# Attention's products with V: one run per pair of heads over all queries, and attention's tiles in rings

## The chip, the cores and the metric

The kernel runs on one core of a Trainium2 chip. The metric is the time of one execution on the device in microseconds (us); smaller is better. Executions are timed several times, and the median is given.

Five engines take part, each with its own instruction queue: TensorE (PE; its weight loads are shown as PEld), VectorE (DVE), ScalarE (ACT), GpSimd (POOL) and SyncE (SP), which here only issues DMAs.

## The reference

```
# q, k, v: (4, 8, 576, 64) float32      B, H, S, D
# M_prev: (4, 8, 64, 64), z_prev: (4, 8, 64), beta: (8,)
scores = q @ k^T / sqrt(D), causal mask
a      = softmax(scores)
local  = a @ v
q_p    = phi(q)                          # phi(x) = elu(x) + 1
mem    = (q_p @ M_prev) / (q_p @ z_prev + 1e-6)
g      = sigmoid(beta)                   # one per head
x      = g * mem + (1 - g) * local       # -> (2304 tokens, 512)
h = x @ w1_in;  y   = (h * cos(h))  @ w1_out       # 512 -> 2048 -> 512
h = y @ w2_in;  out = (h * tanh(softplus(h))) @ w2_out
```

The four weight matrices of the two FFNs come as float64, everything else as float32.

## The kernel before

**Attention.** The eight heads of a batch make four pairs, so there are 16 pairs of heads (B = 4, NP = 4). A pair's queries are done in NQ = 5 steps of 128 (the last has 64 queries, of both heads at once). The generator `attention` goes through all 80 steps, and each step passes three stages, LAGB = 2 and LAGC = 4 steps apart:

- `stage_a`: the scores of the step's queries with all keys up to them (L238, one matmul for each head, in rows 0 to 63 and 64 to 127 of the array; L251 for the last step), into the PSUM tiles sp and sd. DVE adds the mask and takes the minimum (L240, L253, L256), ACT takes the exponential and its sum (L243, L258), DVE the reciprocal (L263), and POOL or another engine scales by it and by the gate (L265). The result is the tile at.
- `stage_b`: PE transposes at, 128 keys at a time, with the identity matrix into the PSUM tile tp (L297; L303 into td for the last 64 keys of the last step). `scaled` (L112) copies tp to SBUF as aT (td as aD), on ACT (L115) and DVE (L117) in turn, in the first batch on ACT alone.
- `stage_c`: the output of the step, transposed (64 values of each of the two heads in the partitions, queries in the columns), in the PSUM tile o: the memory's term by a product with the identity (L313), then for each chunk c of 128 keys up to the diagonal and each head j a product of V with aT (L324), which fills the half j of the array's columns. ACT rounds o to float32r in xH (L328), DVE takes the rest in xL (L329); after the last step both are stored (L331, L332).

`memory` makes a pair's memory term (L277 on PE into mp, L280 to L282 on DVE, result mo) ahead of its first step. `prep` issues a pair's loads on SP's queue (kd L204, qd L206, mz L209, vt L212, qt L215) and is called at step PREP = 3 of the pair before.

A plain float32 matmul is two records of PE in the trace. A product in float32r is one record.

**The FFNs.** `ffn` is a generator of units: L420 makes h from x's two float32r parts and the weights' two, ACT, DVE and POOL make cos (L367 to L376, split in L391 and L392), and `mm2_t` makes y (L478). Tokens of a batch can start once the batch's attention has been stored. The first FFN's first half of d_ff is laid among attention's steps from the second batch on; its second half follows, then the second FFN (mish, `mm2_n`, L487). The weights are converted from float64 by `to_f32` (L121, on POOL, ACT and DVE), beginning at step CONV0 = 14 of attention.

**What sets the order.** The program is written as these generators; the scheduler of the Tile framework then sets each engine's order from the program's dependences, the buffers of each pool (BUFS) and estimates of its own. Attention's PSUM tiles have the tags S (scores) and T (all else) of one pool. A tile of a tag with n buffers waits for the release of the tile n before it.

In the trace, attention's first batch lasts to 87.7 us, where the first L420 stands; up to 131 us the first weights are still being converted; from there to 380 us attention and the first FFN's first half go side by side. The first FFN ends at 682 us, and the second takes the rest.

## Time and profile before

| what | value |
|---|---|
| time, median of 3 runs | 1071.06 us (1069.19 to 1071.45) |
| span of the profiled execution | 1068.0 us, 17139 instructions |
| PE busy | 1042.6 us (98%) |
| DVE busy | 490.7 us (46%) |
| ACT busy | 485.8 us (45%) |
| POOL busy | 391.6 us (37%) |

The profile is of one execution, whose own time is its span, 1068.0 us; the timed runs are others, and their median lies 3.1 us above the span. Busy time is the union of an engine's instructions in the trace; engines work side by side, so the shares don't add up. The rows further down give the line of the kernel, the engine, the operation and the tiles: `o<-aT,vt` is a matmul that writes o and reads aT and vt. The shape after it, as 128\*64, is the part of the array that the matmul fills, rows by columns.

### The profile page before, as it was taken

What the parts mean: (1) busy time and instruction counts of PE and PEld (TensorE: products, weight loads), DVE (VectorE), ACT (ScalarE), POOL (GpSimd) and SP (SyncE); (2) the same over time, 40 slices, a digit from 0 to 9 for tenths busy, and PEclk for the clock granted to TensorE, in tenths of its full rate; (3) what the DMA queues carried; (4) which work ended last, traced back from release to release, by engine and by line L of the source; (5) the groups of instructions that cost most, each with busy time, mean ns of one, the idle gap of its engine ahead of it and who ended that gap; (6) DMA issues with size and microseconds to landing.
All of it is one profiled execution on the core that took longest, in us unless ns stands there. A gap on an engine that the chain in (4) does not pass through costs nothing.

```text
span 1068.0 us, 17139 instructions
## 1 busy us (share of the span) xinstructions
PE 1042.6 (98%) x6512; PEld 873.7 (82%) x6512; DVE 490.7 (46%) x1136; ACT 485.8 (45%) x1023; POOL 391.6 (37%) x425
## 2 busy tenths in 40 slices
PE   6997999999999999999999999999999999999998
PEld 4666688787878899998888889888888888888897
DVE  4588885445554558776766655665000000000000
ACT  6797875556564534344535454543322321222131
POOL 3377853323232334555555555654101010110100
PEclk8999999999999999999999999999999999999999
DMA  6366642323121275425345355630300300110010
GB/s 235 119 196 224 205 135 82 119 83 122 59 87 46 73 266 190 139 90 198 110 166 177 111 176 185 228 119 22 116 1 1 118 1 0 60 40 1 21 41 20
DMA packets 66369, 116.99 MB, mean 110 GB/s; under 512 B 5616, under 2 KB 25072, under 8 KB 66288
## 3 DMA queue, kind: packets, MB, share of 16 engines
q1 hardware_dynamic: 66288, 115.91, 32.2%
q8 instruction: 51, 0.84, 0.3%
q14 instruction: 30, 0.25, 0.1%
HBM read 87.58 MB, written 28.31 MB: 109 GB/s over the span
## 4 chain that ended last, share of the span: by engine, by line
PE 92%; ACT 2%; DVE 2%; DMA 2%; issue 1%; POOL 1%; SPq 0%; DVEq 0%; POOLq 0%; ACTq 0%
PE h L420 37%; PE y L478 20%; PE y L487 18%; PE o L324 5%; PE sp L238 4%; PE tp L297 4%; PE o L313 2%; PE mp L277 1%; PE sp L251 1%; DMA qt<-in_qp_dram 1%; DMA wst<-in_w1i_dram 1%; DVE at L240 1%; ACT at L243 1%; DMA vt<-in_vn_dram 1%; POOL at L265 0%
## 5 line engine op out<-in xcount | busy, mean ns | idle before, releaser
L420 PE MATMUL h<-xbH,w 128*128 128x256 f32 (+1 forms) x1536 | 393.0, 338 | 0.1
L420 PEld LDWEIGHTS h<-xbH,w 128*128 128x128 f32 x1536 | 266.9, 190 | 33.7 <-issue 1.0
L420 PE MATMUL h<-xbL,w 128*128 128x256 f32 (+1 forms) x768 | 258.0, 336 | 1.5 <-DMA xbL<-xsL 1.5
L478 PE MATMUL y<-g,w 128*128 128x256 f32 (+1 forms) x1344 | 221.5, 319 | 4.4 <-ACT aT L115 4.2
L478 PEld LDWEIGHTS y<-g,w 128*128 128x128 f32 x1344 | 193.1, 192 | 30.8 <-issue 9.4
L487 PE MATMUL y<-w,g 128*128 128x512 f32 x864 | 201.8, 389 | 0.0
L487 PEld LDWEIGHTS y<-w,g 128*128 128x128 f32 x864 | 161.9, 188 | 33.5
L392 DVE TENSOR_TENSOR g<-e,g 128x512 fp32r<-128x512 f32 x36 | 24.9, 691 | 297.1 <-ACT g L115 297.1
L420 PEld LDWEIGHTS h<-xbL,w 128*128 128x128 f32 x768 | 145.6, 190 | 16.9 <-DMA xbL<-xsL 1.7
L392 POOL TENSOR_TENSOR g<-e,g 128x512 fp32r<-128x512 f32 x36 | 47.8, 1328 | 286.5 <-ACT g L115 286.5
L265 POOL TENSOR_SCALAR at<-at,sm,omg 128x128 f32<-128x128 f32 (+2 forms) x144 | 102.7, 723 | 134.4 <-DVE sm L263 119.2
L384 ACT ACTIVATE e<-h 128x512 f32<-128x512 f32 x72 | 43.0, 597 | 232.5 <-PE h L420 231.0
L392 POOL TENSOR_TENSOR g<-u,g 128x512 fp32r<-128x512 f32 x72 | 102.0, 1436 | 121.5 <-ACT g L115 45.6
L367 ACT ACTIVATE u<-h 128x512 int32<-128x512 f32 x72 | 42.9, 595 | 111.9 <-PE h L420 104.2
L243 ACT ACTIVATE at<-at,mn 128x128 f32<-128x128 f32 (+3 forms) x128 | 70.9, 555 | 28.2 <-DVE mn L240 26.8
L129 DVE SCALAR_TENSOR_TENSOR wst<-wst 128x512 int32<-128x512 int32 x64 | 53.9, 843 | 37.7 <-POOL wst L119 31.3
L119 POOL TENSOR_SCALAR wst<-wst 128x512 f32<-128x512 f32 x64 | 46.4, 731 | 63.2 <-DMA wst<-in_w1i_dram 25.1
L297 PE MATMUL tp<-ident,at 128*128 128x128 f32 x384 | 63.9, 285 | 5.6 <-DVE den L281 2.2
L368 DVE SCALAR_TENSOR_TENSOR u<-u,h 128x512 f32<-128x512 int32 x72 | 49.0, 682 | 40.8 <-ACT u L367 40.5
L240 DVE CUSTOM_DVE_ANT_0 at<-sp,mask 128x128 f32<-128x128 f32 (+3 forms) x128 | 59.3, 482 | 17.6 <-PE sp L238 16.0
L133 DVE TENSOR_TENSOR wst<-wst 128x512 int32<-128x512 int32 x64 | 66.1, 1035 | 1.2
L324 PE MATMUL o<-aT,vt 128*64 128x128 f32 (+1 forms) x896 | 64.5, 272 | 1.7 <-ACT aT L115 1.5
(76 smaller groups left out, 1084.1 us busy)
## 6 DMA issues: line engine op xcount, KB each, us to landing
wst<-in_w1i_dram SPq DMA_DIRECT2D x16, 512.0 KB, 5.4
wst<-in_w1o_dram SPq DMA_DIRECT2D x16, 512.0 KB, 4.6
wst<-in_w2i_dram SPq DMA_DIRECT2D x16, 512.0 KB, 4.0
wst<-in_w2o_dram SPq DMA_DIRECT2D x16, 512.0 KB, 4.7
qd<-in_qT_dram SPq DMA_DIRECT2D x16, 320.0 KB, 3.4
vt<-in_vn_dram SPq DMA_DIRECT2D x16, 320.0 KB, 3.2
xbH<-xsH SPq DMA_DIRECT2D x20, 256.0 KB, 4.9
xbL<-xsL SPq DMA_DIRECT2D x20, 256.0 KB, 4.6
```

Source lines behind the costliest of these rows:

```text
L129: nc.vector.scalar_tensor_tensor(lo, hi, 3, lo, ALU.logical_shift_left, ALU.bitwise_or)
L133: nc.vector.tensor_tensor(dst, lo, hi, ALU.bitwise_xor)
L240: nc.vector.tensor_tensor_reduce(at[:, :N], sp[:, :N], mask[:, SM - q0:SM - q0 + N], SSC, 3.0e38, ALU.add, ALU.min, mn[:, j:j + 1])
L243: marks["act"] = nc.scalar.activation(at[:, :N], at[:, :N], AF.Exp, bias=mn[:, j:j + 1], scale=-1.0, accum_out=sm[:, j:j + 1]).ins
L265: turn_of("sc", b == 0).tensor_scalar(at[:, :N], at[:, :N], sm[:, j:j + 1], gates[j], ALU.mult, ALU.mult)
L297: nc.tensor.transpose(tp[:, c:c + P], at[:, c:c + P], ident)
L324: marks["pe"] = nc.tensor.matmul(o[j * D:(j + 1) * D, :n], st["vt"][:kk, c, j * D:(j + 1) * D], a, start=False, stop=c == i, skip_group_ch ...
L368: nc.vector.scalar_tensor_tensor(u, u.bitcast(I32), -TWO_PI, h, ALU.mult, ALU.add)
L392: turn_of(kind).tensor_tensor(gL, g, gH.bitcast(F32), ALU.subtract)
L420: nc.tensor.matmul(h[:, a * T:(a + 1) * T], w_[:, c, f0:f0 + P], x_[c], start=m == 0, stop=m == 3 * NC - 1)
L478: nc.tensor.matmul(y[e // per][:, cols], w_[:, f, es], g_, start=fst and m == 0 and e % per == 0, stop=lst and m == 2, skip_group_check=True)
L487: nc.tensor.matmul(y[t], g_[:, tsl], w_[:, f, :], start=fst and m == 0, stop=lst and m == 2, skip_group_check=True)
```

## The change

The product with V is made once for each pair of heads, after its last step, and no longer in each step. For each chunk c of 128 keys, one matmul for each head takes all queries from the diagonal on: 512, 448, 320, 192 and 64 columns (L341 of the new kernel). The first 64 queries lie in a bank of their own, od, with a memory term (L327) and one product for each head (L334) of their own. The memory term of the rest is five products with the identity (L331). Two evacuations on each of ACT and DVE follow, of 64 and of 512 columns, and the two stores.

For this the transposed weights of a whole pair are kept: aTr holds two turns of two heads, in place of the seven aT buffers. The last step's transposes, which hold both heads, go into it by two copies, one for each head (ACT and DVE in turn).

The tiles kd, qd, vt, qt, ph, xH, xL and at are now each one tile with slots that are taken in turn (`ring`), and the buffers of kd, qd, aD and mo go from four to two, those of xL from three to two. The scheduler is free to set another order.

```diff
 BUFS = dict(
-    mb=2, kd=4, qd=4, aD=4, vt=2, qt=1, ph=2, den=2, mo=4, xH=1, xL=3, sm=7, mn=2, at=8, aT=7, u=2, e=3, g=4, h=4, y=4, xb=3, yp=3, yh=2, yl=2, wst=2, S=6, T=8,
+    mb=2, kd=2, qd=2, aD=2, vt=2, qt=1, ph=2, den=2, mo=2, xH=1, xL=2, sm=7, mn=2, at=8, u=2, e=3, g=4, h=4, y=4, xb=3, yp=3, yh=2, yl=2, wst=2, S=6, T=8,
 )
...
+    rings = {}
+
+    def ring(pool, tag, shape, dtype=F32):
+
+        if tag not in rings:
+            rings[tag] = [pool.tile([shape[0], BUFS[tag], *shape[1:]], dtype, name=tag), 0]
+        r = rings[tag]
+        r[1] += 1
+        return r[0][:, (r[1] - 1) % BUFS[tag]]
 
...
+        aTr = ap.tile([P, 4, NQ - 1, S], F32, name="aTr")
...
-            kd = ap.tile([P, S], F32, tag="kd", name="kd", bufs=BUFS["kd"])
+            kd = ring(ap, "kd", [P, S], F32)
...
-            vt = ap.tile([P, NQ, P], F32, tag="vt", name="vt", bufs=BUFS["vt"])
+            vt = ring(ap, "vt", [P, NQ, P], F32)
...
         def stage_b(b, p, i):
             st = prepd[b, p]
-            n = P if i < 4 else D
-            aTs = []
-            for at in st["at", i]:
+            if i == 0:
+                r = turns["aT"] = (turns.get("aT", -1) + 1) % 2
+                st["aT"] = [aTr[:, 2 * r + h] for h in range(2)]
+                st["aD"] = ap.tile([P, 2, D], F32, tag="aD", name="aD", bufs=BUFS["aD"])
+            aT = st["aT"]
+            W = min(i + 1, 4)
+            for j, at in enumerate(st["at", i]):
                 tp = bank("T", [P, SM], "tp")
-                aT = ap.tile([P, SM], F32, tag="aT", name="aT", bufs=BUFS["aT"])
-                W = P * min(i + 1, 4)
-                for c in range(0, W, P):
-                    nc.tensor.transpose(tp[:, c:c + P], at[:, c:c + P], ident)
-                scaled("aT", aT[:, :W], tp[:, :W], first=b == 0)
-                aTs.append(aT)
+                for c in range(W):
+                    nc.tensor.transpose(tp[:, c * P:(c + 1) * P], at[:, c * P:(c + 1) * P], ident)
+                tc4 = tp.rearrange("k (c q) -> k c q", q=P)[:, :W]
+                if i < 4:
+                    scaled("aT", aT[j][:, :W, i * P:(i + 1) * P], tc4, first=b == 0)
+                else:
+                    for h in range(2):
+                        scaled("aT", aT[h][:, :, SM:], tc4[:, :, h * D:(h + 1) * D], first=b == 0)
             if i == 4:
-                aD = ap.tile([P, 2, D], F32, tag="aD", name="aD", bufs=BUFS["aD"])
                 tp = bank("T", [P, SM], "td")
                 nc.tensor.transpose(tp[:D, :P], at[:, SM:], ident)
-                scaled("aD", aD.rearrange("p a b -> p (a b)")[:D, :P], tp[:D, :P])
-                aTs.append(aD)
-            st["aT", i] = aTs
-
-        def stage_c(b, p, i):
+                scaled("aD", st["aD"].rearrange("p a b -> p (a b)")[:D, :P], tp[:D, :P])
+
+        def stage_c(b, p):
             st = prepd[b, p]
-            n = P if i < 4 else D
-            q0 = i * P
-            o = bank("T", [P, P], "o")
-            nc.tensor.matmul(o[:, :n], st["mo"][:, i], ident[:, P - n:], start=True, stop=False,
-                             skip_group_check=True)
-            for c in range(i + 1):
-                kk = P if c < 4 else D
+            aT, aD, vt = st["aT"], st["aD"], st["vt"]
+            od = bank("T", [P, D], "od")
+            o = bank("T", [P, SM], "o")
+            nc.tensor.matmul(od, st["mo"][:, 0], ident[:, :D], start=True, stop=False, skip_group_check=True)
+            for c in range(NQ):
+                r0, n = (D, D) if c == 0 else (0, P) if c < 4 else (0, D)
+                i0 = r0 if c < 4 else P - D
+                nc.tensor.matmul(o[:, c * P + r0 - D:c * P + r0 - D + n], st["mo"][:, c], ident[:, i0:i0 + n],
+                                 start=c == 0, stop=False, skip_group_check=True)
+            for j in range(2):
+                nc.tensor.matmul(od[j * D:(j + 1) * D, :], vt[:D, 0, j * D:(j + 1) * D], aT[j][:D, 0, :D],
+                                 start=False, stop=True, skip_group_check=True)
+            for c in range(NQ):
+                q0 = max(c * P, D)
                 for j in range(2):
-                    if i < 4:
-                        a = st["aT", i][j][:, c * P:(c + 1) * P]
-                    elif c < 4:
-                        a = st["aT", i][0][:, c * P + j * D:c * P + (j + 1) * D]
-                    else:
-                        a = st["aT", i][1][:D, j]
+                    kk = P if c < 4 else D
+                    a = aT[j][:, c, q0:] if c < 4 else aD[:D, j]
                     marks["pe"] = nc.tensor.matmul(
-                        o[j * D:(j + 1) * D, :n], st["vt"][:kk, c, j * D:(j + 1) * D], a,
-                        start=False, stop=c == i, skip_group_check=True).ins
-            xH = st["xH"]
-            nc.scalar.activation(xH[:, q0:q0 + n], o[:, :n], AF.Copy)
-            nc.vector.tensor_tensor(st["xL"][:, q0:q0 + n], o[:, :n], xH[:, q0:q0 + n].bitcast(F32), ALU.subtract)
-            if i == 4:
-                nc.sync.dma_start(xsH[p, :, b * S:(b + 1) * S], xH.bitcast(F32))
-                marks["sp"] = nc.sync.dma_start(xsL[p, :, b * S:(b + 1) * S], st["xL"].bitcast(F32)).ins
-                del prepd[b, p]
+                        o[j * D:(j + 1) * D, q0 - D:], vt[:kk, c, j * D:(j + 1) * D], a,
+                        start=False, stop=c == NQ - 1, skip_group_check=True).ins
+            xH, xL = st["xH"], st["xL"]
+            for t, q0, q1 in ((od, 0, D), (o, D, S)):
+                nc.scalar.activation(xH[:, q0:q1], t, AF.Copy)
+                nc.vector.tensor_tensor(xL[:, q0:q1], t, xH[:, q0:q1].bitcast(F32), ALU.subtract)
+            nc.sync.dma_start(xsH[p, :, b * S:(b + 1) * S], xH.bitcast(F32))
+            marks["sp"] = nc.sync.dma_start(xsL[p, :, b * S:(b + 1) * S], xL.bitcast(F32)).ins
+            del prepd[b, p]
 
...
             if 0 <= s - LAGC < ns:
-                stage_c(*steps[s - LAGC])
+                if steps[s - LAGC][2] == NQ - 1:
+                    stage_c(*steps[s - LAGC][:2])
```

The new lines that the prediction names: L249 and L262 are the scores (L238 and L251 before), L310 the transposes (L297), L331 and L327 the memory term (L313), L341 and L334 the products with V (L324), L438 the first FFN's h (L420), L505 the second FFN's y (L487). The number of L324's 480 matmuls becomes 192.

**The order on PE, in the first pairs.** Before, at the first pair of heads, transposes of softmax weights into tp, the memory term (`o<-ident,mo`) and the products with V (`o<-aT,vt`) take turns, a step at a time:

```order
L297 MATMUL tp<-ident,at 128x128 x6
L313 MATMUL o<-ident,mo 128x128
L324 MATMUL o<-aT,vt 64x128
L297 MATMUL tp<-ident,at 128x128 x3
L324 MATMUL o<-aT,vt 64x128
L297 MATMUL tp<-ident,at 128x128 x3
L313 MATMUL o<-ident,mo 128x128
L324 MATMUL o<-aT,vt 64x128 x4
L297 MATMUL tp<-ident,at 128x128 x8
L277 MATMUL mp<-mz,ph 128x130 x5
```

In the new kernel a whole pair's products stand in one run, and a long run of transposes behind it:

```order
L310 MATMUL tp<-ident,at 128x128 x2
L327 MATMUL od<-ident,mo 128x64
L334 MATMUL od<-aTr,vt 64x64 x2
L331 MATMUL o<-ident,mo 128x64
L331 MATMUL o<-ident,mo 128x128 x3
L331 MATMUL o<-ident,mo 128x64
L341 MATMUL o<-aTr,vt 64x512 x2
L341 MATMUL o<-aTr,vt 64x448 x2
L341 MATMUL o<-aTr,vt 64x320 x2
L341 MATMUL o<-aTr,vt 64x192 x2
L341 MATMUL o<-aD,vt 64x64 x2
L310 MATMUL tp<-ident,at 128x128 x18
```

What stood between the transposes now stands behind them, and the transposes of the next pair, which need only free banks and the scaled weights, have moved together.

**The order on PE, among the first FFN's matmuls.** Before, between two groups of L420 (not shown) stood pieces of two steps:

```order
L297 MATMUL tp<-ident,at 128x128 x4
L303 MATMUL td<-ident,at 64x128
L238 MATMUL sp<-kd,qd 128x256 x2
L313 MATMUL o<-ident,mo 128x128
L324 MATMUL o<-aT,vt 64x128 x8
L297 MATMUL tp<-ident,at 128x128 x2
L238 MATMUL sp<-kd,qd 128x384 x2
L313 MATMUL o<-ident,mo 128x64
L324 MATMUL o<-aT,vt 64x64 x8
L324 MATMUL o<-aD,vt 64x64 x2
```

Here is one of the new runs, with the scores (`sp`, `sd`) of the last step of the next pair in it:

```order
L331 MATMUL o<-ident,mo 128x64
L341 MATMUL o<-aTr,vt 64x512
L310 MATMUL tp<-ident,at 128x128 x4
L262 MATMUL sp<-kd,qd 128x512
L262 MATMUL sd<-kd,qd 128x64
L341 MATMUL o<-aTr,vt 64x512
L341 MATMUL o<-aTr,vt 64x448 x2
L341 MATMUL o<-aTr,vt 64x320 x2
L341 MATMUL o<-aTr,vt 64x192 x2
L341 MATMUL o<-aD,vt 64x64 x2
L249 MATMUL sp<-kd,qd 128x128 x2
L249 MATMUL sp<-kd,qd 128x256 x2
```

The two heads' products of 512 columns, which would lie side by side in the array, are parted by the transposes and the scores; the products of the other chunks stand together.

**The order on DVE, at a last step's copies.** DVE copies half of the aT tiles. Before, after the first batch, the copy of a last step's tile waits for PE alone (in brackets the engines whose signals an instruction waits for), and the score reductions (`at,mn<-sp,mask`) and the conversion of weights (wst) stand behind it:

```order
L117 COPY aT<-tp 128x512 [waits PE_49]
L117 COPY aD<-td 64x128 [waits PE_49]
L329 TENSOR_TENSOR xL<-o,xH 128x128 [waits Activation_49]
L282 TENSOR_TENSOR mo<-mp,den 128x384 [waits DVE_49]
L282 TENSOR_TENSOR mo<-mp,den 128x256 [waits DVE_49]
L263 RECIPROCAL sm<-sm 128x2 [waits Activation_49]
```

In the new kernel DVE copies one head's half (128x4x64) of the last step's tile:

```order
L126 COPY aD<-td 64x128 [waits PE_49]
L139 TENSOR_SCALAR wst<-wst 128x512 [waits DVE_49]
L251 ISA at,mn<-sp,mask 128x512 [waits PE_49]
L251 ISA mn 128x1
L274 RECIPROCAL sm<-sm 128x2 [waits Activation_49]
L126 COPY aTr<-tp 128x4x64 [waits Activation_49]
L251 ISA at,mn<-sp,mask 128x512 [waits PE_49]
L251 ISA mn 128x1
L142 TENSOR_TENSOR wst<-wst 128x512 [waits DVE_49]
```

That copy waits for ACT, which copies the other head's half of the same bank ahead of it. On SP's queue the second pair's qt moves from the 16th place to the 13th.

## Rows read from the trace of the kernel before

**Rows 1.** The page: busy time of the engines; the chain that ended last, by engine.

```profile
PE 1042.6 (98%) x6512; PEld 873.7 (82%) x6512; DVE 490.7 (46%) x1136; ACT 485.8 (45%) x1023; POOL 391.6 (37%) x425
...
PE 92%; ACT 2%; DVE 2%; DMA 2%; issue 1%; POOL 1%; SPq 0%; DVEq 0%; POOLq 0%; ACTq 0%
```

**Rows 2.** Stretches: length, busy PE, PEld, DVE, ACT, POOL; granted clock; DMA share, GB/s.

```profile
24.00:87.00 63.00, 61.85 (x504) 41.88 (x503) 47.65 (x179) 52.62 (x165) 33.70 (x44) 1.00 0.50 160
87.00:131.00 44.00, 36.88 (x298) 27.68 (x294) 37.50 (x117) 33.32 (x88) 34.11 (x37) 0.96 0.62 207
131.00:380.00 249.00, 244.82 (x2088) 204.71 (x2085) 134.82 (x455) 142.69 (x361) 82.23 (x107) 0.99 0.28 89
380.00:682.00 302.00, 301.75 (x1786) 269.42 (x1785) 204.70 (x269) 136.30 (x198) 161.42 (x140) 1.00 0.49 169
100.00:105.00 5.00, 1.84 (x20) 1.30 (x19) 5.00 (x13) 4.97 (x9) 1.80 (x2) 0.98 0.41 120
104.00:109.00 5.00, 4.17 (x40) 3.47 (x40) 5.00 (x14) 3.06 (x7) 3.85 (x3) 0.66 0.42 118
```

**Rows 3.** PE's waits, 0 to 170 us: total us, times, longest.

```profile
PE sp L238 <- DMA kd<-in_kT_dram: 4.5, 1, 4.5
```

**Rows 4.** PE's waits, 170 to 440 us.

```profile
PE y L478 <- ACT aT L115: 4.2, 3, 1.4
```

**Rows 5.** The timeline of PE, 298 to 303 us: start, length, records.

```profile
298.44 0.49 PE L313 MATMUL o<-ident,mo 128*128 128x128 f32 x2
298.86 1.09 PE L324 MATMUL o<-aT,vt 128*64 128x128 f32 x16
299.89 0.44 PE L297 MATMUL tp<-ident,at 128*128 128x128 f32 x2
300.25 0.92 PE L238 MATMUL sp<-kd,qd 64*128 64x384 f32 x4
301.10 0.43 PE L313 MATMUL o<-ident,mo 128*128 128x64 f32 x2
301.47 0.69 PE L324 MATMUL o<-aT,vt 128*64 128x64 f32 x16
302.08 0.33 PE L324 MATMUL o<-aD,vt 64*64 64x64 f32 x4
```

**Rows 6.** The timeline of PE, 41.5 to 52 us.

```profile
42.23 0.88 PE L324 MATMUL o<-aT,vt 128*64 128x128 f32 x12
43.04 0.66 PE L297 MATMUL tp<-ident,at 128*128 128x128 f32 x4
...
45.35 0.91 PE L238 MATMUL sp<-kd,qd 64*128 64x384 f32 x2
46.19 0.43 PE L313 MATMUL o<-ident,mo 128*128 128x64 f32 x2
...
50.55 0.44 PE L324 MATMUL o<-aT,vt 128*64 128x128 f32 x4
50.92 1.12 PE L251 MATMUL sp<-kd,qd 128*128 128x512 f32 x2
```

**Rows 7.** The timeline of all engines, 199 to 205 us.

```profile
200.06 1.28 ACT L243 ACT_TABLE_LOAD   x1
...
201.35 0.72 ACT L243 ACTIVATE at<-at,mn 128x512 f32<-128x512 f32 x1
...
202.94 0.47 ACT L115 ACTIVATE aT<-tp 128x384 f32<-128x384 f32 x1
...
203.46 1.79 PE L478 MATMUL y<-g,w 128*128 128x256 f32 x8 [1.39 <-ACT aT L115]
```

**Rows 8.** Groups of instructions: number | busy us, mean ns | idle before, releaser.

```profile
L324 PEld LDWEIGHTS o<-aT,vt 128*64 128x64 f32 x896 | 44.7, 139 | 14.9 <-ACT aT L115 3.6 <-issue 1.7 <-ACT xH L328 0.8
L329 DVE TENSOR_TENSOR xL<-o,xH 128x128 fp32r<-128x128 f32 (+1 forms) x80 | 21.4, 272 | 23.2 <-ACT xH L328 22.8
L328 ACT ACTIVATE xH<-o 128x128 fp32r<-128x128 f32 (+1 forms) x80 | 20.1, 256 | 16.4 <-PE o L324 14.8 <-PE h L420 1.0 <-DMA xsH<-xH 0.3
```

More of the change, by code (lines that the diff above doesn't have):

```diff
@@ L195, in bank @@
             return pools[0].tile(shape, F32, tag=tag, name=name, bufs=BUFS[tag])
+        aTr = ap.tile([P, 4, NQ - 1, S], F32, name="aTr")
+        turns = {}
         pairs = [(b, p) for b in range(B) for p in range(NP)]
@@ L201, in prep @@
             st = {}
-            kd = ap.tile([P, S], F32, tag="kd", name="kd", bufs=BUFS["kd"])
+            kd = ring(ap, "kd", [P, S], F32)
             nc.sync.dma_start(kd, kT[b, p])
-            qd = ap.tile([P, S + D], F32, tag="qd", name="qd", bufs=BUFS["qd"])
+            qd = ring(ap, "qd", [P, S + D], F32)
             nc.sync.dma_start(qd, qT[b, p])
@@ L210, in prep @@
             st["mz"] = mz
-            vt = ap.tile([P, NQ, P], F32, tag="vt", name="vt", bufs=BUFS["vt"])
+            vt = ring(ap, "vt", [P, NQ, P], F32)
             nc.sync.dma_start(vt, vn[b, p])
             st["vt"] = vt
-            qt = ap.tile([P, S], F32, tag="qt", name="qt", bufs=BUFS["qt"])
+            qt = ring(ap, "qt", [P, S], F32)
             nc.sync.dma_start(qt, qp[b, p])
-            ph = ap.tile([P, S], F32, tag="ph", name="ph", bufs=BUFS["ph"])
+            ph = ring(ap, "ph", [P, S], F32)
             nc.scalar.activation(ph, qt, AF.Relu, scale=-1.0)
@@ L220, in prep @@
             st["ph"] = ph
-            st["xH"] = ap.tile([P, S], F32R, tag="xH", name="xH", bufs=BUFS["xH"])
-            st["xL"] = ap.tile([P, S], F32R, tag="xL", name="xL", bufs=BUFS["xL"])
+            st["xH"] = ring(ap, "xH", [P, S], F32R)
+            st["xL"] = ring(ap, "xL", [P, S], F32R)
             prepd[b, p] = st
@@ L231, in stage_a @@
             mn = ap.tile([P, 2], F32, tag="mn", name="mn", bufs=BUFS["mn"])
-            ats = [ap.tile([P, S], F32, tag="at", name="at", bufs=BUFS["at"]) for _ in range(2 if i < 4 else 1)]
+            ats = [ring(ap, "at", [P, S], F32) for _ in range(2 if i < 4 else 1)]
             if i < 4:
```

## The prediction

> **What bounds the kernel now.** I read the page first. TensorE (PE) is busy 98% of the span, and the chain that ended last is 92% PE [rows 1]. A busy PE is not yet the bound, so I went to the stages. From 24 to 87 us PE idles 1.1 us of 63, from 131 to 380 us it idles 4.2 of 249, from 380 to 682 us 0.3 of 302 [rows 2]. Only from 87 to 131 us, where the first weights are converted, it idles 7.1 of 44, and there DVE is busy 37.5 and POOL 34.1 us. So in three of the four stretches whatever PE no longer does comes off the end; in the fourth it may turn into waiting. The list of PE's waits agrees: at the start 4.5 us for the first keys [rows 3], in 170 to 440 us only 4.2 us, three waits of 1.4 us each for an ACT copy of transposed weights (aT) [rows 4].
>
> Then I read attention's work on PE row by row, to see what its time is made of. All its matmuls but the transposes are plain float32, which PE runs as two records. A V-product fills half of the array's columns (128\*64 in the rows), the two heads' products start together, and so do the two heads' scores (64\*128, half of the rows).
>
> From start to start a run of 16 records lasts 1.03 us [rows 5], one of 12 lasts 0.81, one of 4 lasts 0.37 [rows 6]. Four more records (both heads, 128 columns) therefore cost **0.22 us**, and a run pays 0.15 us beside. The run of 16 records with 64 columns lasts 0.61 us [rows 5]: less the 0.15 that is 0.115 per four records, half of 0.22. Time follows the columns streamed, so weight loads, whose length doesn't depend on them, are hidden inside a run.
>
> **The price of a change of shape.** From the start of the L313 at 298.44 to that at 301.10 us are 2.66 us [rows 5]. Streaming alone is 0.22 (L313) + 0.87 (16 records) + 0.22 (two transposes, taken as 128 columns each like L313's records) + 0.66 (scores, 384 columns, both heads) = 1.97. The other 0.69 us are four changes between the full array and a half: 0.17 each. From V's side: 0.15 in the run, and L313 ahead of the run of 16 takes 0.42 in place of 0.22, of which I give half to the change before it: 0.25 to 0.35 for two changes. I take **0.16 us**, with 0.13 and 0.175 as bounds.
>
> **The price of a half alone.** One head's score of 384 columns by itself lasts 0.84 us, from 45.35 to 46.19 [rows 6]; both heads together lasted 0.85 [rows 5]. So where the order parts the two heads, the second costs as much again: 0.22 us for each 128 columns.
>
> **The change on PE.** Its products stream the same columns: per head 1,600 of V (before 128 x (1+2+3+4) + 64 x 5; after 64 + 512 + 448 + 320 + 192 + 64), and 576 of the memory term, in six matmuls in place of five. Eighteen V matmuls per pair of heads go, 288 in all; by the 64-column run that is worth nothing by itself. What moves is how often the array changes shape and how often heads are parted; both are counted in the two orders.
>
> - Changes of shape: 290 before, 219 after. 71 x 0.16 = **-11.4 us** (-9.2 to -12.4).
> - Scores whose heads are parted: 12 pairs with 4,096 columns before, 18 with 6,144 after. 2,048 / 128 x 0.22 = **+3.5 us**.
> - V-products parted: 6 with 768 columns before; after, 5 of 512 columns and 2 of 64. 1,920 / 128 x 0.22 = **+3.3 us**; the order shown with the change has one such place, where transposes and scores stand between the two products of 512.
>
> Sum on PE: -4.6 us.
>
> **The other engines.** Each pair's five evacuations on ACT and five on DVE become two and two. ACT's 80 xH take 0.26 us each, DVE's 80 xL 0.27 [rows 8]: 20.1 and 21.4 us. After: per pair one of 64 columns (at most the mean, 0.26) and one of 512, which I bound by 0.26 and 0.7, the length of ACT's 512-wide exponentials [rows 7]. At 0.7, 15.4 us each: some 5 us less on either engine. The copies of step 4's transposes become two per pair; sixteen more at 0.47 (a 384-wide copy [rows 7]) are 7.5 us over ACT and DVE at most. PE's busy rows cover all of this; uncovered, between 87 and 131 us, it is at most a quarter of either, under 2 us, of both signs. I take nothing.
>
> The rings with fewer buffers (kd, qd 4 to 2) let SP issue the third pair's keys only after the first pair's last score; behind them in SP's queue stand the next qt, mz and kd, and PE's memory term waits for these. V's next load waits for a longer run of products than before. Work for at least one whole pair lies between such an issue and its need: I take nothing, and bound it by the one such wait that the trace shows, 4.5 us [rows 3]. On the other side the second pair's qt now stands 13th in SP's queue, not 16th: a gain of nothing, or of up to the 4.5 us of [rows 3] at the start, which I leave in a rival.
>
> **A new wait.** DVE's half of step 4's copy now waits for ACT's half of the same bank, and PE's first long product needs both. Behind DVE's copy stand its score reductions and weight conversions; behind PE's product stands everything. ACT's queue can be long: from the table load at 200.06 to the aT copy that PE waited for, 3.4 us pass [rows 7]. In the new order two to five us of PE work mostly lie between those transposes and the product that needs them, so I price it at nothing in the sum.
>
> **Two rules weighed against the rows.** The 64-column run halves with its columns [rows 5], so loads don't show. The Trainium skill (TensorE: Matmul & The Clock Gate, "What overlaps and what doesn't") says that a weight load overlaps running matmuls only where its row group differs; the two heads share theirs, so no load would be hidden. By it the 576 loads that go would save more: 896 such loads are 44.7 us of load time [rows 8], 576 of them 29 us, and the sum would be near -33. By the rows it stays -4.6. I give the rule 0.03.
>
> The granted clock is 1.00 from 24 to 87 us [rows 2], in which transposes stand among everything else, and it dips to 0.66 from 104 to 109 us, after PE had worked 1.84 of the 5 us before [rows 2]. The same page ("PE-mode transpose") says that transposes don't count as activity for the clock; the new order has runs of 16 and 18 of them where the old had 8 at most. No run of that length is in this trace.
>
> **Rivals.**
> 1. *Swallowed.* Ahead of the first FFN matmul the array changes shape 83 times before and 71 after, though one more pair's scores stand there now. So much of the saving falls into attention's first batch, which feeds the stretch from 87 to 131 us, where PE waits for converted weights. If it waits as much longer as it was sooner there, 4.6 us shrink to 2 or nothing: 1069 to 1073. For it: DVE 85% busy there. Against: PE's idle is 1.1 us in the 63 us before, so PE's work sets when that stretch is reached.
> 2. *Slower: the run stands for its copies.* Each pair's run has one place to stand, for the ACT-then-DVE copy, at about 1.4 us, the length of the three waits in [rows 4]. Four such waits more than now eat the 4.6 us, five make it slower by over 0.2%; at nine of sixteen runs it is 12.6 - 4.6 = 8 us slower, 1079. For it: five of the new order's runs are broken up at just this product. Against: ACT sits idle over 40% of 131 to 380 us [rows 2].
> 3. *More.* The three waits of [rows 4] were for banks behind ACT's table loads; a new order can lose them (-4.2), and start sooner: 1058 to 1062.
> 4. *Clock.* If a long run of transposes brings the clock to half as at 104 us, a dip costs 0.34 x 5 = 1.7 us; with one in each of four early pairs 6.8 - 4.6 = +2.2: 1073.
>
> **How the numbers follow.** The span before is 1068.0 us; the median of the timed runs is 3.1 us above it. 1068.0 - 4.6 = 1063.4; with the 3.1 that is **1066.5 us**. Chances: the sum as it stands 0.42 (by its bounds 1064 to 1069); swallowed 0.22; slower 0.15; more 0.14; clock 0.04; loads (some 1040) 0.03. A measurement tells 0.2%, some 2 us, from no change. Faster: 0.40 of the first, with "more" and "loads", 0.57. Slower: "slower", a little of "swallowed" and of "clock", 0.20. The same: 0.23. The range from 1058 to 1076 leaves out the loads and the far part of "slower".
>
> **What would show it.** Two heads' products of 512 columns in 0.9 us, together; attention's last product and the last stage's first matmul (L505) some 5 us earlier; changes of shape at 0.16 us. Wrong would be: PE waits on aTr at L341; heads' products that follow each other, which would be 2.75 us more per pair, 44 in all; more idle between the first FFN matmuls.

## The result, and the profile after

The changed kernel takes **1079.86 us** (median of 4 runs, 1078.54 to 1081.43), the kernel before 1071.26 us (4 runs beside it). The ratio is **1.0081, interval 1.0065 to 1.0098**: 8.6 us slower, where 4.6 us faster was forecast, and outside the range from 1058 to 1076. The profiled execution of after has a span of 1079.2 us, 11.2 us more than that of before.

The page of after, its engines and its chain, beside [rows 1]:

```profile
span 1079.2 us, 16070 instructions
PE 1047.4 (97%) x5968; PEld 860.8 (80%) x5968; DVE 496.2 (46%) x1094; ACT 479.2 (44%) x983; POOL 391.9 (36%) x425
...
PE 82%; DVE 5%; DMA 5%; POOL 3%; ACT 3%; issue 2%; SPq 0%; POOLq 0%; DVEq 0%; ACTq 0%
```

PE has 4.8 us more busy time for less work, and 10% of the chain has moved from PE to the engines that it waits for. The stretches of [rows 2] say where (length, busy PE, PEld, DVE, ACT, POOL, granted clock, DMA share, GB/s; the last cut at 420 and 478 us):

```profile
24.00:87.00 63.00, 59.74 (x360) 37.52 (x359) 42.58 (x162) 49.16 (x154) 33.01 (x44) 0.92 0.46 146
87.00:131.00 44.00, 41.50 (x260) 28.41 (x259) 36.41 (x111) 28.94 (x81) 25.34 (x30) 0.92 0.64 206
131.00:380.00 249.00, 245.22 (x1733) 193.21 (x1732) 140.47 (x435) 143.03 (x339) 91.15 (x113) 0.99 0.31 99
...
420.00:478.00 58.00, 50.94 (x394) 49.96 (x393) 49.34 (x63) 21.32 (x30) 30.84 (x29) 0.94 0.41 125
```

The same 58 us of before:

```profile
420.00:478.00 58.00, 57.75 (x457) 56.33 (x456) 42.54 (x69) 21.82 (x32) 32.13 (x33) 1.00 0.41 139
```

Read two columns together, PE's busy time and the granted clock. From 24 to 131 us PE is busy 2.5 us more than before, but at 0.92 of the clock and not at 1.00 and 0.96. The table sums windows of half a us in the two executions. Idle is the window less PE's busy time. What the clock takes is an estimate: busy time times what the clock lacks of 1.

| us | before | after | difference |
|---|---|---|---|
| last product with V starts | 379.2 | 380.1, with 5 more FFN matmuls (0.6) done | +0.3 at equal work |
| of it PE idle | 21.5 | 20.7 | -0.8 |
| of it lost to the clock | 6.2 | 11.9 | +5.7 |
| the rest: PE's work at full clock | 351.6 | 347.5 - 0.6 | **-4.7** |
| 380 to 480 us: idle and clock | 0.2 + 0 | 7.5 + 3.1 | **+10.4** |

In these two executions PE's work shrank by about what was forecast (4.6), attention ended no sooner, and 10.4 us were lost where no line of the code was changed: the first FFN behind attention. L505 starts at 693.3 us, before (L487) at 682.0.

The loss behind attention is the larger, and e1 below takes most of it away. The figures for attention hold for these two executions only. PE's order in e1, e10 and e14 below is that of after, record for record, until well past the last product with V. There the last product starts at 380.2, 374.9 and 376.4 us, the clock takes 12.1, 5.6 and 8.2 us, and the rest is 347.4, 349.5 and 348.5 us. The rows of e10 for the first two stretches, to be read beside those of after above; then the last product of e10 and that of after (each with the lines of its own kernel):

```profile
24.00:87.00 63.00, 59.51 (x377) 38.17 (x376) 45.00 (x172) 51.49 (x162) 34.53 (x46) 0.97 0.53 163
87.00:131.00 44.00, 41.39 (x258) 28.63 (x257) 37.88 (x116) 29.83 (x80) 27.09 (x31) 0.96 0.62 199
```

```profile
374.81 0.33 PE L350 MATMUL o<-aD,vt 64*64 64x64 f32 x4
```

```profile
379.96 0.33 PE L341 MATMUL o<-aD,vt 64*64 64x64 f32 x4
```

So one order on PE ended attention anywhere from 0.4 us later than before to 4.9 us sooner at equal work, and most of the difference is the clock. The execution of before was itself one with little lost to the clock: its mean granted clock was 0.993, where the runs of before beside the experiments have 0.991 on the mean.

The waits of PE from 0 to 380 us in after (total, times, longest):

```profile
PE tp L310 <- DVE mn L251: 4.4, 4, 2.3
PE tp L310 <- DVE mo L293: 3.3, 1, 3.3
PE o L341 <- ACT aTr L124: 2.9, 1, 2.9
...
PE od L327 <- ACT aTr L124: 0.8, 1, 0.8
```

Of sixteen runs of products one stood for its copy (L341), and one stood at its start for a bank that ACT's copy frees (L327), not nine. The three waits of [rows 4] are gone. From 380 to 700 us:

```profile
PE y L496 <- POOL g L410: 5.0, 4, 2.4
PE y L496 <- DVE g L126: 2.2, 1, 2.2
```

Before, one wait of 0.2 us stood there. The largest, on POOL's timeline (start, length) and then on PE's:

```profile
463.94 0.66 POOL L128 TENSOR_SCALAR wst<-wst 128x512 f32<-128x512 f32 x1 [4.03 <-DMA wst<-in_w1i_dram]
467.99 0.64 POOL L128 TENSOR_SCALAR wst<-wst 128x512 f32<-128x512 f32 x1 [3.39 <-DMA wst<-in_w1o_dram]
468.59 0.65 POOL L128 TENSOR_SCALAR w<-wst 128x512 fp32r<-128x512 f32 x1
469.20 1.70 POOL L410 TENSOR_TENSOR g<-u,g 128x512 fp32r<-128x512 f32 x1
```

```profile
468.17 0.36 PE L496 MATMUL y<-g,w 128*128 128x256 f32 x1 [2.17 <-DVE g L126]
470.95 8.58 PE L496 MATMUL y<-g,w 128*128 128x256 f32 x47 [2.43 <-POOL g L410]
```

POOL stands 3.39 us in front of a weight piece that has not landed; the split of g (L410) stands behind it in POOL's queue, and PE's y behind that. The order of POOL's instructions at this place, before and after:

```
before                                   after
L119 TENSOR_SCALAR wst<-wst x2           L128 TENSOR_SCALAR wst<-wst x2
L119 TENSOR_SCALAR w<-wst                L128 TENSOR_SCALAR w<-wst
L163 TENSOR_TENSOR w<-wst,w              L410 TENSOR_TENSOR g<-u,g
L392 TENSOR_TENSOR g<-u,g x2             L172 TENSOR_TENSOR w<-wst,w
                                         L410 TENSOR_TENSOR g<-u,g
```

Before, this group repeats from 429 to 482 us and the two splits follow the pieces together; after, the last step of a piece stands between the two. The code there is the same.

### The profile page after: what moved, and what is told of

Same layout as the page of the kernel before. It is cut to its first block, busy times and chain, and to the rows that moved or that the text cites. A ratio compares the mean times of both kernels' runs of the same rounds, so it can differ in the third digit from the quotient of the medians.

```text
span 1079.2 us, 16070 instructions
## 1 busy us (share of the span) xinstructions
PE 1047.4 (97%) x5968; PEld 860.8 (80%) x5968; DVE 496.2 (46%) x1094; ACT 479.2 (44%) x983; POOL 391.9 (36%) x425
## 4 chain that ended last, share of the span: by engine, by line
PE 82%; DVE 5%; DMA 5%; POOL 3%; ACT 3%; issue 2%; SPq 0%; POOLq 0%; DVEq 0%; ACTq 0%
PE h L438 33%; PE y L505 18%; PE y L496 16%; PE o L341 4%; PE sp L249 4%; PE tp L310 3%; DMA wst<-in_w1i_dram 3%; DMA wst<-in_w1o_dram 2%; PE o L331 1%; POOL at L276 1%; PE mp L288 1%; DVE wst L138 1%; DVE wst L139 1%; PE sp L262 1%; POOL w L172 1%
## 5 line engine op out<-in xcount | busy, mean ns | idle before, releaser
L438 PE MATMUL h<-xbH,w 128*128 128x256 f32 (+1 forms) x1536 | 392.2, 338 | 1.4 <-DVE mo L293 1.0
L438 PEld LDWEIGHTS h<-xbH,w 128*128 128x128 f32 x1536 | 266.1, 189 | 38.2 <-DVE wst L139 2.0
L438 PE MATMUL h<-xbL,w 128*128 128x256 f32 (+1 forms) x768 | 258.1, 336 | 0.0
L505 PE MATMUL y<-w,g 128*128 128x512 f32 x864 | 201.8, 389 | 0.0
L505 PEld LDWEIGHTS y<-w,g 128*128 128x128 f32 x864 | 161.9, 188 | 33.4
L410 DVE TENSOR_TENSOR g<-e,g 128x512 fp32r<-128x512 f32 x36 | 25.9, 719 | 289.1 <-ACT g L124 289.1
L438 PEld LDWEIGHTS h<-xbL,w 128*128 128x128 f32 x768 | 145.6, 190 | 15.1
L410 POOL TENSOR_TENSOR g<-e,g 128x512 fp32r<-128x512 f32 x36 | 47.3, 1314 | 276.9 <-ACT g L124 276.9
L410 POOL TENSOR_TENSOR g<-u,g 128x512 fp32r<-128x512 f32 x72 | 102.2, 1436 | 108.8 <-ACT g L124 38.4
L254 ACT ACTIVATE at<-at,mn 128x128 f32<-128x128 f32 (+3 forms) x128 | 71.4, 560 | 22.0 <-DVE mn L251 18.3
L137 ACT ACTIVATE wst<-wst,c_seven 128x512 int32<-128x512 uint32 x64 | 49.2, 770 | 68.6 <-DMA wst<-in_w1o_dram 19.5
L249 PE MATMUL sp<-kd,qd 64*128 64x256 f32 (+3 forms) x256 | 67.4, 502 | 5.3 <-DMA kd<-in_kT_dram 4.7
L251 DVE CUSTOM_DVE_ANT_0 at<-sp,mask 128x128 f32<-128x128 f32 (+3 forms) x128 | 59.7, 484 | 27.1 <-PE sp L249 14.7
L310 PE MATMUL tp<-ident,at 128*128 128x128 f32 x384 | 62.2, 286 | 9.2 <-DVE mn L251 4.4
```

The lines of the kernel that those rows point to most:

```text
L137: nc.scalar.activation(lo, lo.bitcast(U32), AF.Relu, scale=-(2.0 ** -29), bias=c_seven)
L249: nc.tensor.matmul(sp[:, :N], st["q"][rows, q0:q0 + P], st["k"][rows, :N], start=True, stop=True)
L251: nc.vector.tensor_tensor_reduce(at[:, :N], sp[:, :N], mask[:, SM - q0:SM - q0 + N], SSC, 3.0e38, ALU.add, ALU.min, mn[:, j:j + 1])
L254: marks["act"] = nc.scalar.activation(at[:, :N], at[:, :N], AF.Exp, bias=mn[:, j:j + 1], scale=-1.0, accum_out=sm[:, j:j + 1]).ins
L310: nc.tensor.transpose(tp[:, c * P:(c + 1) * P], at[:, c * P:(c + 1) * P], ident)
L410: turn_of(kind).tensor_tensor(gL, g, gH.bitcast(F32), ALU.subtract)
```

## Experiments on the stretch behind attention

**e1: the changed kernel with the old order there.** Edges of order (which make an instruction queue behind another and wait for nothing) chain the 208 instructions of POOL, DVE and ACT behind attention's last store; ORDER lists them as the kernel before issues them.

```diff
+    for e, order in ORDER.items():
+        ins = [i for i in traced if i.engine == getattr(mybir.EngineType, e)]
+        for a, b in zip(order, order[1:]):
+            tc.add_manual_dep(ins[b], ins[a].name, mybir.DependencyInfo(
+                mybir.DependencyClass.NoSync, mybir.DependencyReason.DATA), reason="order")
```

> The changed kernel, with POOL, DVE and ACT made to issue their 208 instructions behind attention's last store (conversion of the second half of the first weights, the first FFN's cosine and split) in the order in which the kernel before issues them. Nothing else differs. Theory A: the 10.9 us that the changed kernel loses between 420 and 478 us come from that order, which the change moved along without touching the code; attention itself is neither faster nor slower. Then 1079.9 - 10.5 = about 1069.5, between 1068 and 1071.5. Rival B: the new run of products is what is slow (its waits, its evacuations, fewer buffers), and what is seen behind attention is its aftermath: then 1078 to 1081.

Measured: 1073.99 us, ratio 1.0016 (1.0000 to 1.0032). Of the 0.81% some 0.65% go, about 7 us, with nothing touched but the order of unchanged instructions. Theory A holds in part: the time lies above its 1068 to 1071.5 and well under rival B's 1078 to 1081. PE still idles 2.2 us there and the clock lacks 1.7. (The expectation speaks of 10.9 us lost in this stretch; by the rows shown it is 7.1 of idle and 3.1 of clock.)

```profile
420.00:478.00 58.00, 55.84 (x427) 54.41 (x426) 38.86 (x65) 20.49 (x29) 27.92 (x29) 0.97 0.39 120
```

**e2: the kernel before with the new order there.** The same edges, with the list of the changed kernel.

> The other way round: the kernel before, with POOL, DVE and ACT made to issue the same 208 instructions behind attention in the order in which the changed kernel issues them. Theory A: PE waits for the split of g as it does in the changed kernel, 1071.3 + 10 = 1079 to 1083. Rival B: the order is harmless where attention is the old one, 1070 to 1073.

Measured: 1073.52 us, 1.0021 (1.0006 to 1.0036): some 2 us slower, far from the 10 of theory A and more than B's none. The order costs 2 us beside the old attention and 7 beside the new: so the order alone is not the whole cause. That its cost hangs on when loads and units arrive in it is a guess; no run settles it.

**e14, e10, e15: all five engines, and an earlier load.** e14 adds PE and SP to the list; e10 also lets the first two loads of weights go ahead of the last stores; e15 does that to the kernel before.

```diff
-    with tc.issue_after(marks["pe"]), tc.issue_after(marks["sp"]):
+    with tc.issue_after(marks["pe"]):
```

> The changed kernel with the order of the kernel before on all five engines behind attention, as e10, but the first loads of weights behind the last stores. Theory A: the conversion's later start is what e1 still lost: as e1, 1072 to 1075. Rival: it was the order on PE and SP: as e10, 1068 to 1071.

> The changed kernel with the order behind attention of the kernel before on all five engines, and the first two loads of weights of that stretch ahead of the last two pairs' stores on SP's queue. In e1 (three engines' order) 4.5 to 5 us were still lost behind attention, waits and the half clock behind one of them. Theory A: they come from the conversion starting 0.8 us later against PE (first load at 382.2, before at 381.4 us), so that each load lands after POOL's turn: with the earlier load the stretch loses under 2 us, 1068 to 1072. Rival (what is lost there has another source): as e1, 1072 to 1076.

> The kernel before with its own order behind attention, and the first two loads of weights ahead of the last pairs' stores, as in e10. Its trace shows 0.2 us of waiting behind attention, so there is nothing to gain: 1069 to 1072. Were it faster than that, e10 would owe its gain to the load and not to a loss that it takes back.

Measured: e14 1072.19 us, 1.0010 (0.9995 to 1.0026); e10 1069.96 us, 1.0000 (0.9983 to 1.0017); e15 1071.75 us, 1.0004 (0.9989 to 1.0019). The load by itself gives the kernel before nothing. The changed kernel comes level with before; e1, e14 and e10 lie within each other's intervals, so which of the two edits took the last 4 us is not resolved. The times of e14 and e10 lie in the ranges of their theories A.

**e5, e6: a third staging slot**, order left free.

```diff
-    mb=2, kd=2, qd=2, aD=2, vt=2, qt=1, ph=2, den=2, mo=2, xH=1, xL=2, sm=7, mn=2, at=8, u=2, e=3, g=4, h=4, y=4, xb=3, yp=3, yh=2, yl=2, wst=2, S=6, T=8,
+    mb=2, kd=2, qd=2, aD=2, vt=2, qt=1, ph=2, den=2, mo=2, xH=1, xL=2, sm=7, mn=2, at=8, u=2, e=3, g=4, h=4, y=4, xb=3, yp=3, yh=2, yl=2, wst=3, S=6, T=8,
```

> The changed kernel with three staging slots for weights in conversion (wst) in place of two; the order is left free. Theory A: behind attention POOL stands in front of a weight piece whose load was issued late because both slots were taken, and the split of g, for which PE waits, stands behind it in POOL's queue. A third slot lets the load run ahead: the 10.9 us between 420 and 478 us shrink to 3 or less, 1069 to 1073. Rival (the conversion's own work on DVE and POOL is what is too long, not its slots): 1077 to 1081.

> The kernel before with three staging slots, as the other side of e5. The trace of before shows no wait behind attention that a third slot could take away, and PE's work in attention is 1.6 us less in the new order as I count it: 1068 to 1073 by either theory.

Measured: e5 1080.88 us, 1.0078 (1.0060 to 1.0096); e6 1084.76 us, 1.0110 (1.0092 to 1.0128). Both expectations of mine fell. With one more buffer the scheduler set another order everywhere: the last product of e6 starts at 385.7 us (before 379.2), and behind it 6.5 us more go to idle and clock. The pair says nothing of slots. A small edit moved this kernel by 13 us; that its order did it is not shown here, since no run holds e6's order, but e13 below shows it for another edit.

## Experiments on the parts of the change

**e9: rings alone.** The tiles and buffers of the change (kd, qd, aD, mo and xL at two, aT kept at seven), with stage_b and stage_c as before and the old order behind attention.

```diff
...
-            kd = ap.tile([P, S], F32, tag="kd", name="kd", bufs=BUFS["kd"])
+            kd = ring(ap, "kd", [P, S])
```

> The kernel before with only the second half of the change: kd, qd, vt, qt, ph, xH, xL and at as rings, two buffers of kd, qd, aD and mo, two of xL; the products with V are the old ones, a step at a time, and the order behind attention is that of the kernel before on POOL, DVE and ACT. If the rings cost nothing, as I priced them: 1070 to 1074. If the fewer buffers are what makes PE wait in attention: 1076 to 1081. I count 1.5 us more work on PE in the new order.

**e13: the same with the old order** on PE, DVE, ACT and POOL, all instructions, by the edges of e1.

> e9's kernel (rings and fewer buffers, products a step at a time), with every instruction of PE, DVE, ACT and POOL in the order of the kernel before; SP's loads are ordered freely. Theory A: fewer buffers make nothing wait; what made e9 9 us slower is the other order that they led to. Then as the kernel before, 1069 to 1073. Rival: a load or a tile of the rings comes free too late: 1076 to 1082.

Measured: e9 1080.59 us, **1.0090** (1.0073 to 1.0107); e13 1070.43 us, **0.9991** (0.9978 to 1.0004). These two are the clearest pair of the study: same instructions, same tiles, same buffers, ten us apart by order. Beside products a step at a time, rings and fewer buffers cost nothing, as priced; what they led the scheduler to do cost as much as the whole change. In e9 the loss lies in attention, whose last product starts at 388.5 us; PE waits between 87 and 160 us:

```profile
PE sp L253 <- DVE mo L297: 3.0, 1, 3.0
PE tp L312 <- POOL wst L134: 2.0, 1, 2.0
```

With the same buffers and the old order neither stands in e13, so a scarcity of tiles alone does not make them.

**e3: the run in pieces of 128 columns.**

```diff
+                for e0 in range(q0, S, P):
+                    e1 = min(e0 + P, S)
...
-                    a = aT[j][:, c, q0:] if c < 4 else aD[:D, j]
+                        a = aT[j][:, c, e0:e1] if c < 4 else aD[:D, j]
```

> The changed kernel with the order of e1, and each product with V cut into pieces of at most 128 columns, still in one run per pair: 480 matmuls with V in place of 192. If PE's time in the run goes by the columns streamed and weight loads are hidden (my working): as e1 within 3 us, 1066 to 1072. If a weight load does not overlap the matmul before it in the same rows of the array (the Trainium skill, TensorE: Matmul & The Clock Gate, What overlaps and what doesn't): 288 more matmuls of two loads each, 576 x 0.05 = 29 us more, near 1098.

Measured: 1078.48 us, 1.0060 (1.0039 to 1.0081), 4.5 us over e1, more than the 3 I allowed and far from 29. The scheduler set another order in attention here too, so the times alone do not judge the loads; the rows do. A whole run in pieces, and the same run of after:

```profile
254.74 2.75 PE L350 MATMUL o<-aTr,vt 128*64 128x128 f32 x52
257.42 0.33 PE L350 MATMUL o<-aD,vt 64*64 64x64 f32 x4
```

```profile
249.76 2.69 PE L341 MATMUL o<-aTr,vt 128*64 128x512 f32 x16
252.38 0.33 PE L341 MATMUL o<-aD,vt 64*64 64x64 f32 x4
```

From start to start 52 records take 2.68 us and 16 take 2.62: the 576 more weight loads cost some 1 us over all sixteen runs. The Trainium skill (TensorE: Matmul & The Clock Gate, "What overlaps and what doesn't") would have had them unhidden; the trace disagrees. Over e3's twelve runs the clock takes 17.4 us of the span (an estimate: span times one less the mean granted clock), over e1's 12.4; that is the difference in time, and what is left is 1058.6 and 1059.5 us.

**e4: the run two steps later.**

```diff
-LAGC = 4
+LAGC = 6
```

> The changed kernel with the order of e1, and stage_c six steps behind stage_a in place of four (LAGC 6), so that each pair's run of products is called for two steps later, long after its copies. In the order 199 changes of shape are left of 219, and parted heads cost less (16 us of doubled streaming in place of 28, as I count it): PE's work up to attention's end is 10.8 us less than in e1. Theory A: waits for the copies ahead of the run, and the half clock behind them, go too, and PE's work comes off the end: 1055 to 1062. Rival (the waits only move, to the next instruction whose turn it is): 1066 to 1071.

Its products take the V of the pair two further on, since the ring of two slots is refilled ahead of them. Measured: 1076.79 us, 1.0052 (1.0033 to 1.0070). Slower than e1, with 10.8 us less to do on PE by my count: theory A falls, and the rival's mechanism holds, at a time above its 1066 to 1071. The waits moved to the transposes (for POOL's scaling, for copies and for the memory's divisor), the last product started at 381.9 us (e1 380.2), and the clock lacks 16.7 us over its runs.

```profile
PE tp L317 <- POOL at L283: 4.9, 6, 3.1
...
PE tp L317 <- ACT aTr L131: 3.8, 3, 2.4
PE tp L317 <- DVE den L299: 3.5, 2, 2.8
```

**e7, e8: no conversion of weights**, in the changed kernel and in the one before (`dst = hi` in place of the five operations).

> The changed kernel with the conversion of the weights from float64 left out: the upper half of each float64 is taken as a float32, so POOL, ACT and DVE lose five instructions for each of 64 pieces. Loads and splits stay. To be read against e8. Theory A: the new run of products saves PE's time, and in the changed kernel waits for DVE, ACT and POOL, which convert weights at the same time, take it back. Without that work PE is the only bound, and e7 is faster than e8 by most of the 9.7 us by which its work on PE is less as I count it from the two orders: 5 to 10 us. Rival (a run that stands for all of a pair's copies is slow by itself, whatever the other engines do): e7 as slow as e8 or slower.

> The kernel before with the same conversion left out, for e7 to be read against. PE's idle 7 us between 87 and 131 us and some 2 us of half clock there can go: 1055 to 1066.

Measured: e7 1069.23 us, e8 1064.17 us (0.9977 and 0.9925 of before). Theory A falls: without any conversion the new order is still 5 us slower. To the last product, e7's trace has 6.8 us less work on PE than e8's, 1.8 us more idle, and 6.3 us more lost to the clock. The runs agree: on their mean the clock takes 18.3 us of e7 and 7.6 of e8, and what is left is 1049.5 and 1054.7 us. One stretch shows the clock, e7 and then e8:

```profile
24.00:36.00 12.00, 12.00 (x32) 6.69 (x32) 5.20 (x23) 6.41 (x21) 1.68 (x3) 0.50 0.15 38
```

```profile
24.00:36.00 12.00, 12.00 (x103) 8.70 (x102) 8.31 (x35) 10.26 (x32) 4.09 (x7) 0.96 0.23 69
```

PE is busy all 12 us in both. At half clock it gets through 32 records and not 103, in part because these are wider ones; the share of busy time alone would not tell the two apart. In e7 the clock had been at half since 15.5 us; PE waited 3.1 us until 19.3 us, for the divisor, and has worked since on scores, memory products and transposes.

**e11, e12: transposes of a fixed tile**, so that PE doesn't wait for softmax.

```diff
-                    nc.tensor.transpose(tp[:, c * P:(c + 1) * P], at[:, c * P:(c + 1) * P], ident)
+                    nc.tensor.transpose(tp[:, c * P:(c + 1) * P], fixed[:, c * P:(c + 1) * P], ident)
```

> e1's kernel, with the transposes reading one fixed tile in place of the softmax's weights: PE no longer waits for the minimum, the exponential and the scaling, which are all still done; copies, products and conversion stay. To be read against e12. Theory A: the new order's half clock (10 us of it between 24 and 150 us) follows PE's waits for softmax and copies. With hardly a wait left the clock stays up and the work saved shows: e11 faster than e12 by 4 to 8 us. Rival (long stretches of transposes and scores without products with V let the clock fall even where PE doesn't wait): e11's mean granted clock stays at or under 0.988, and e11 is no faster than e12.

> The kernel before with the transposes reading the same fixed tile, and its own order behind attention. For e11 to be read against. 1062 to 1069 by either theory: PE's waits for softmax go, those for converted weights between 87 and 131 us stay.

Measured: e11 1072.14 us (1.0016), e12 1066.15 us (0.9963): e11 is 6 us slower, and its granted clock 0.990 against 0.994. The rival's half on the time holds, its reason not quite: e11 did not get rid of its waits. PE idles 23.5 us up to 700 us against 16.6 in e12. Of the difference 3.6 us lie in attention, where the two longest waits of transposes (3.1 and 3.0 us, for DVE) can only be for banks, as they read a fixed tile; 3.3 lie behind it, where e12 has none. That the run of products asks more of these queues at one place is argued and not shown.

**e16: heads side by side.** The second head's copy comes later, so its product is put first and the first head's made to follow it.

```diff
-                for j in range(2):
-                    kk = P if c < 4 else D
+                kk = P if c < 4 else D
+                pair = []
+                for j in (1, 0):
                     a = aT[j][:, c, q0:] if c < 4 else aD[:D, j]
-                    marks["pe"] = nc.tensor.matmul(
+                    with (tc.issue_after(pair[0]) if pair else ExitStack()):
+                        marks["pe"] = nc.tensor.matmul(
...
+                    pair.append(marks["pe"])
```

> e10's kernel with the second head's product ahead of the first's in each chunk, and the first made to follow it in PE's queue: the copy for the second head is the later one, so where it is there, both are, and the products lie side by side. In the order 208 changes of shape are left of 219, and parted heads (scores' too) stream 21.7 us, before 27.8; I count 6.6 us less of PE's work than in e10. Theory A (PE's work comes off the end where PE is what the stretch waits for): 1063 to 1067, faster than the kernel before by 0.4 to 0.8%. Rival (what PE no longer does turns into waiting for softmax and copies, and into half clock, in attention's first 150 us): 1069 to 1073, as e10.

Measured: **1067.78 us, 0.9974** (0.9956 to 0.9991): 0.26% faster than the kernel before, and the only one of the study that does all the work and beats both. It lies between the ranges of theory A and of the rival, so neither is met. It is e10 with less work on PE: 8.0 us under before in the trace, by the sums of the table (I had counted 4.6 + 6.6 = 11.2). Of these, 2.6 us come off the end (the kernel before took 1070.38 us beside it). Its interval and e10's overlap.

## Why the prediction was wrong

**The sum on PE had the right sign and about the right size.** -4.6 was forecast. Against before's 351.6 us the traces with the changed kernel's order give, less 0.6 for the five FFN matmuls, -4.7 (after), -4.8 (e1), -3.7 (e14) and -2.7 (e10). The rest comes out smaller where more is put down to the clock, so the estimate seems to charge the clock too much; e10, which lost about as much to the clock as before did (5.6 and 6.2 us), is the closest pair. The price of a change of shape (0.16 us) then over-counts, as it did by some 40% where the difference was larger (e7 9.7 counted, 6.8 found; e16 11.2 and 8.0). With the bounds of this price the sum is -2.4 to -5.6, which gives 1065.5 to 1068.7 and not 1064 to 1069. The run of the four chunks, shown at e3, reads as priced: from start to start 2.62 us; 1,472 columns of both heads at 0.22 for 128 and 0.15 for the run make 2.68. The evacuations of 512 columns took 0.595 us on ACT and 0.688 on DVE, inside the bounds of 0.26 and 0.7.

**The step that failed** is the first: "in three of the four stretches whatever PE no longer does comes off the end". It took PE's idle time of before (0.3 us of 302 in [rows 2]) for a property of the stretch. It was a property of that order. The stretch from 380 to 682 us has little room: in 58 us PE waits for a chain through POOL and DVE that also converts weights, and another order of the same work loses 10.4 us. No term stood in the sum for it, since I counted only PE's instructions and only those that the diff touches. With the old order there e1 takes some 7 us of it back. Of the signs that the prediction named for being wrong, waits for aTr at L341 came once (2.9 us), and more idle between the first FFN matmuls is what decided. The orders on POOL, DVE and ACT behind attention were there to be compared; they differ in 25 of 48, 71 of 108 and 28 of 52 places.

**The second term that was missing** is the clock, 5.7 us in attention and 3.1 behind it in these two executions. As an estimate over runs it is less in attention: the clock takes 16.2 us of after and 9.5 of before, a difference of 6.7; if 3.1 of it stand behind attention, as in the profile, 3.6 are left for attention. I had a rival for it, at 0.04 and for the wrong reason: long runs of transposes. The longest run of transposes, eighteen of them, is here (PE's timeline), and the window around it:

```profile
38.08 2.18 PE L310 MATMUL tp<-ident,at 128*128 128x128 f32 x18
```

```profile
37.00:42.00 5.00, 5.00 (x49) 4.20 (x45) 2.31 (x11) 3.81 (x13) 0.50 (x2) 1.00 0.53 169
...
61.00:67.00 6.00, 5.96 (x24) 4.07 (x26) 3.15 (x15) 3.57 (x14) 5.33 (x7) 0.50 0.07 27
```

The clock is full through it. In the second window it is at half (0.50, the lower of the two levels, 1.2 GHz). About that fall stand two waits for DVE's minimum, 0.57 and 1.61 us, which end at 58.74 and 61.05 us; ahead of that at 142.5 us, 2.94 us for aTr; ahead of that at 470 us, 2.17 and 2.43 us for g. Each of these falls costs 1.7 us or 3.1 to 3.2 on top of the wait. The waits do not fix the fall: in e10 the same two waits for the minimum (0.56 and 1.61 us) stand ahead of the same run, and from 64.5 to 68 us its granted clock is 1.00 again, where after stays at 0.50 to 67.5.

**Rival 2** came out at the right time, 1079, by luck and with the wrong mechanism: two waits for ACT's copies (3.7 us in all), not nine. **Rival 1** (swallowed) is what attention did in the profiled execution, but not for its reason: from 87 to 131 us PE idles 2.5 us, before 7.1, and the clock took the saving. **Rival 3**'s three waits did go, -4.2, and new ones took their place. **The loads** (some 1040) are refuted by e3. Rings at nothing: right for the buffers (e13), wrong for the order that they brought (e9).

What stays open: why the changed order behind attention costs 7 us beside the new attention and 2 beside the old one, why one order falls to half clock more often in one execution than in another, and why the clock is lower in three pairs with the new products (0.985 against 0.991 in after and before, 0.984 against 0.9935 in e7 and e8, 0.990 against 0.994 in e11 and e12, medians of their runs). In e10 and e14 it is not clearly so: 0.990 in both, with 0.990 and 0.991 in before beside them.

## What to carry to other kernels

Where a scheduler sets the order, an edit is two changes: the edit, and a new order of everything. Compare the orders on all engines, far from the diff too, and hold the order fixed (as e1 and e13 do) before a time is put down to the edit. A busy engine shows what bounds the order at hand. Its idle time does not show how much room another order has: 0.3 us of 302 became 7.5. And one profile of a kernel is one draw: compare several executions of each before microseconds are put down to the clock.

## What was not expected of the hardware

A half clock can outlast the wait ahead of it by far while PE is busy throughout: 12 us of e7 above, and in e3 the 20 us from 85 to 105 us (PE busy 19.84, granted clock 0.50), all scores, memory products, transposes and few products with V. The same kinds of rows run at full clock elsewhere (37 to 60 us in after, granted clock 1.00). The Trainium skill (TensorE: Matmul & The Clock Gate, "PE-mode transpose") says that a transpose doesn't count as a busy PE in the same way; both traces have transposes in such stretches, beside other matmuls, and no run here parts them. Executions of one kernel spread by up to 13 us (e4: 1070.45 to 1083.16; e3: 1071.87 to 1082.97, whose mean granted clock was 0.990 in the fastest and 0.978 in the slowest).
